# One Trainium2 kernel: x in two double loads, w1 in whole columns, and a new order of tasks

## The chip, the cores and the metric

The kernel runs on one core of one Trainium2 chip. Its work is spread over engines that run side by side: PE (TensorE, matrix multiplications; its weight loads are shown as PEld), DVE (VectorE), ACT (ScalarE), POOL (GpSimd) and SP (SyncE, which here only starts transfers). The metric is device time in microseconds, lower is better. A time is the median of several executions; the profile is one more execution, recorded by the hardware profiler.

## The reference

Two branches act on the same x of 2048 tokens by 512 features, in bfloat16, and are mixed by a gate per token:

```python
x = A_x
g = sigmoid((x * gate_w).sum(-1, keepdims=True))
X = rfft2(x)                       # over tokens and features
a = irfft2(X * (w_r + 1j * w_i))   # spectral filter, w of 2048 x 257
h = x @ w1 + b1                    # 512 -> 1792
b = (h * tanh(softplus(h))) @ w2   # 1792 -> 512; the activation is Mish
out = g * a + (1 - g) * b
```

## The kernel before

**Tiles.** x is cut into 16 tiles of 128 tokens; tile t holds the tokens 16p+t for p from 0 to 127. The dense branch goes by four groups c of four tiles and 14 column slices ft of 128 hidden units. Task `m{c}_{ft}` (line 847) is four matmuls of 128x512, one for each quarter of the 512 features, into one PSUM bank; `h{c}_{ft}` (line 852, ACT) applies bias and Mish and so frees the bank. For c = 0 and ft below 4 the task is split in two halves, `ma0_ft` and `m0_ft`, two matmuls each. `n{t}` (line 865) is the second layer for one tile, 14 matmuls; `o{t}` (lines 879, 882) scales it by 1-g.

**The spectral branch.** The transforms are written as matrix products. `bf{a}_0` and `bf{a}_1` (line 586, DVE) add and subtract the two halves of the features of the tiles of one x load. `p{t}` (line 604, PE) transforms along the tokens of a tile, `ep{t}` (line 501 on DVE, 504 on ACT) moves two tiles' results from PSUM to SBUF. `d{g}` (line 619) with `ed{g}` transforms along the features and needs all `ep`. `t{q}` (line 698, 64 small matmuls) combines the 16 tiles, `et{q}{h}` evacuates. The filter follows on DVE: `hp` (line 717), `p1` (720), `ad` (724) with the weights that `w?m`, `w?c`, `w?n` and `w?z` (lines 646 to 671) have spread out in SBUF; `w?n` copies 64x4160, and `wrz1` writes behind `wrn1` and so waits for it. `e1`, `xp`, `ead`, `e2`, `e3` treat one left-over frequency. Then the way back: `it` (line 780) with `eit`, which needs `e3`; `id` (819) with `ec` and `ey` (827, 830); and `ip` (873, 888), which adds the spectral result to the output, for tiles 8 to 15 inside the bank of `n{t}`. `fin` (892) adds the rest, `out` stores.

**The gate.** `graw` loads the gate row; `gt{t}` (line 593, DVE) multiplies it into a tile of x and sums; `zcl`, `ez`, `ez1`, `omg` and `gc` make the factors.

**The front.** `warm` and `fl` are matmuls on constants whose results nobody uses. The first four tiles reach the first layer through PE: `tr{t}` (line 573) transposes, `evx{t}` evacuates. Tiles 4 to 15 are transposed by the transfer `xt{t}`. `tr_b` and `ev_b` do the same for the bias; `tab` makes ACT load the table of Mish.

**What sets the order.** Nothing is scheduled while it runs. `ORDER` (line 329) is one long text; each engine takes its tasks in the order of that text, `name:engine:bank`. An engine may be chosen there, and the digits are PSUM banks (or the slot of a temporary). `place` (line 232) derives from it the waits: on the data, and on the last users of the same bank. So each engine is a queue in which a waiting task holds up all behind it. Loads go out from SP in the order of the text, and each waits until the load six places before it has landed (`KOUT`, line 20). The load groups stand in two constants:

```python
W1P = ((0, 2, 0, 4), (2, 4, 0, 4), (0, 4, 4, 8), (0, 4, 8, 11), (0, 4, 11, 14))   # k0, k1, first slice, end
XP = ((0, 1), (1, 2), (2, 3), (3, 4), (4, 8), (8, 12), (12, 16))
```

`w1_8_0` is the load of w1 for slices 8 to 10, all four feature quarters. In the text of before, the first layer begins with halves of slices 0, 2, 1, then 1 and 2, and then slice 8.

Of the kernel before, what the change touches and what calls it, by code (L numbers as in the profile page):

```python
# [333 lines left out]
p13 bf8_0 ep12:act bf8_1 gt11 m0_13::0 h0_13 m0_11::1 h0_11 wi0s1 m0_12::3 h0_12 p8::6 p9 ep8:act xt10 gt1 p10::4 p11 ep10:dve m1_9::2 h1_9 wr0s2  # L334
m1_12::0 d8::6 d9 xt15 h1_12 xt8 gt8 ed8:act d0::4 d12::2 d13 xt11 ed12:act gt4 xt9 gt9 xt13 gt10 ldM1 wr0s0 m1_4::1 d1 ed0:act wr0s1 d4::6 d5 ed4:act
xt14 m1_13::0 m1_2::2 h1_4 wi1s0 d10::4 d11 ed10:act h1_2 wi1s1 ldM2 d2::6 gt0 d3 m1_8::3 h1_8 m1_5::1 h1_5 gt2 d14::4 gt6 gt15 gt3 zcl d15 ed14:act
wim010:dve m1_3::2 h1_3 ed2:dve m1_10::3 xt12 h1_10 wim011:dve wim000:dve wim001:dve wic0:dve t0::64 d6::1 ez win0:dve h1_13 d7 wr1s0 et00:act
et01:dve wr1s1 m1_0::3 wiz0 hp01_1::1 hp00_1::2 ed6:act m2_2::0 h2_2 hp00_0 h1_0 hp01_0 w2_10 m2_7::6 h2_7 t1::41 et10:act et11:act hp11_0::0 m2_10::7
hp11_1 h2_10 ldM3 m1_1::0 w2_0 m2_5::3 h2_5 wrm000:act m2_0::6 wrm011:dve wrm010:dve ldG2 wrm001:dve wrc0:act c01 m1_7::4 wrn0:dve wrz0 ez1 omg c00
p1_01 m2_9::5 p1_00 m1_6::1 h1_6 h2_0 wim100:dve h1_1 wim101:dve m2_6::2 ad_01 hp10_1::1 m2_3::7 w2_5 ldG0 m2_1::3 h2_1 h2_3 m2_4::1 h2_4 wim111:dve  # L340
m2_11::6 h2_11 hp10_0 h2_6 p1_11 m2_8::0 m1_11::3 h2_8 wim110:dve h2_9 t2::61 et20:act m3_2::0 m2_12::5 m3_6::6 et21:act ad_11 h2_12 m3_1::7 m3_7::1
m2_13::2 p1_10 wic1:act h1_11 wrm111:dve h1_7 wrm101:act wrm100:dve h2_13 m3_12::5 wrm110:dve wrc1:act h3_1 h3_2 m3_0::3 ad_10 wrn1:dve edge ldG1 h3_6
m3_10::4 win1:dve wiz1 ldG3 m3_11::2 h3_11 m3_13::7 h3_0 h3_13 h3_12 wrz1 c02 m3_8::0 hp20_0::0 h3_10 hp20_1 m3_5::6 hp21_0::1 h3_7 m3_9::2 m3_3::3
h3_9 m3_4::7 h3_4 ad_00 hp21_1 p1_21 t3::41 ad_21 et30:act hp30_0::2 n3_0::7 et31:act c03 hp30_1 p1_30 p1_20 h3_3 e1::4 ad_30 xp20::1 h3_8 o3_0:act
ad_20 h3_5 n2_0::5 n0_0::1 xp1::2 xp21 ead::0 e2::2 o0_0:act hp31_1::1 hp31_0 n1_0::3 o1_0:act p1_31 ad_31 rft e3 it5_0::6 it2_0::0 it2_1 it5_1 inv
eit5:act n5_0::4 o5_0:act ezb zt::2 eit2:dve it1_0::0 o2_0:dve it1_1 zte it0_0::6 it0_1 eit0:act zw zr eit1:act it3_0::2 it3_1 eit3:dve n6_0::5
it4_0::6 it4_1 it7_0::3 it7_1 o6_0:dve it6_0::1 it6_1 eit6:act n9_0::0 rfs eit4:dve eit7:act id0::1 id14::6 id15 ec14:act:2 ey14_1 id1 ec0:act:0
id2::4 id3 ec2:act:1 ey0_0 n7_0::3 ey14_0 ey2_0 id10::6 id11 ey2_1 o7_0:act ey0_1 id8::4 id9 ec8:dve:2 ey8_1 id6::1 ec10:act:1 ey10_0 n4_0::3 o4_0:act
ey8_0 ip9_0 ey10_1 id12::4 id7 id13 ec12:dve:0 ey12_1 id4::6 id5 ec4:dve:2 ec6:act:1 n8_0::3 ip8_0 ey6_1 o9_0:act ey6_0 n10_0::0 o8_0:act ey4_0 ip1::1
# [600 lines left out]
```

## Time and profile before

| what | us |
|---|---|
| median of 3 runs | 132.89 (131.75 to 133.75) |
| the profiled execution, its own time | 131.67 |
| its span, first to last instruction | 130.1 |
| PE busy | 124.7 |
| DVE busy | 92.8 |
| ACT busy | 74.0 |
| bytes moved by transfers | 16.88 MB |

The profile tells, for each engine, when an instruction ran and what ended the wait ahead of it. The chain of work that ended last is followed back from the last instruction, at each step to what released it. A line number is that of the kernel's text. Matmuls overlap by their pipeline, so the pitch from start to start is what a matmul costs; its recorded length is longer.

### The profile page before, as it was taken

How to read it: one execution, taken by the hardware profiler on the slowest of the kernel's cores; microseconds unless marked ns; L12 is line 12 of the kernel's file. 1: busy time of each engine (PE TensorE's matmuls, PEld its weight loads, DVE VectorE, ACT ScalarE, POOL GpSimd, SP SyncE). 2: the span in 40 equal slices, each digit the busy share in tenths (PEclk: the TensorE clock that was granted, in tenths of full speed). 3: DMA queues.
4: the chain of work that ended last, by engine and by line, in shares of the span. 5: the costliest groups of instructions: out<-in, count | busy, mean ns of one | idle time of the engine just before them, and what ended most of it. 6: DMA issues, size and time to landing. Idle time of an engine off the chain costs nothing.

```text
span 130.1 us, 2561 instructions
## 1 busy us (share of the span) xinstructions
PE 124.7 (96%) x1076; PEld 65.2 (50%) x1076; DVE 92.8 (71%) x161; ACT 74.0 (57%) x105; POOL 4.7 (4%) x8
## 2 busy tenths in 40 slices
PE   7969999999999999999999999999999999999991
PEld 4624566665654445444454445556645544444440
DVE  0853797999995899999999996337098692803720
ACT  3852989999999879998959024354432520000202
POOL 2000000000470000000000000000000000000000
PEclk9999999999999999999999999999999999999999
DMA  3889998866799969998400002010000002000591
GB/s 109 247 255 367 316 134 282 126 99 67 198 212 140 262 108 292 363 375 274 166 5 0 0 0 55 0 72 10 5 0 0 5 0 81 0 0 0 187 337 40
DMA packets 17302, 16.88 MB, mean 130 GB/s; under 512 B 7628, under 2 KB 14668, under 8 KB 17228
## 3 DMA queue, kind: packets, MB, share of 16 engines
q1 hardware_dynamic: 17120, 16.60, 51.4%
q8 instruction: 8, 0.13, 0.4%
q10 hardware_dynamic: 172, 0.13, 0.3%
q14 instruction: 2, 0.02, 0.1%
HBM read 13.05 MB, written 2.10 MB: 116 GB/s over the span
## 4 chain that ended last, share of the span: by engine, by line
PE 56%; DVE 28%; ACT 5%; DMA 5%; SPq 2%; issue 2%; DVEq 0%
PE ps L865 28%; PE ps L847 14%; DVE rE L724 8%; DVE tmp L717 6%; DMA w_sb<-in_B_w_dram 5%; DVE rC L720 4%; PE ps L819 3%; PE ps L780 3%; PE ps L619 3%; SPq L467 2%; ACT rC L504 2%; DVE rW L649 2%; PE ps L604 2%; DVE rW L661 2%; PE ps L873 1%
## 5 line engine op out<-in xcount | busy, mean ns | idle before, releaser
L847 PE MATMUL ps<-rX,w_sb 128*128 128x512 bf16 x224 | 50.8, 379 | 1.5 <-DMA w_sb<-in_B_w_dram 1.5
L847 PEld LDWEIGHTS ps<-rX,w_sb 128*128 128x128 bf16 x224 | 21.1, 98 | 25.3 <-DMA w_sb<-in_B_w_dram 2.0
L879 ACT ACTIVATE rX<-ps,omg 128x512 bf16<-128x512 f32 x10 | 6.9, 687 | 37.4 <-PE ps L873 22.6
L865 PE MATMUL ps<-w_sb,hs 128*128 128x512 bf16 x112 | 25.2, 379 | 0.0
L852 ACT ACTIVATE hs<-ps,b1f 128x512 bf16<-128x512 f32 x28 | 18.2, 708 | 4.7 <-PE ps L847 3.6
L865 PEld LDWEIGHTS ps<-w_sb,hs 128*128 128x128 bf16 x112 | 10.5, 98 | 11.9
L865 PE MATMUL ps<-w_sb,rD 128*128 128x512 bf16 x56 | 12.8, 379 | 0.0
L865 PE MATMUL ps<-w_sb,rS 128*128 128x512 bf16 x56 | 12.6, 379 | 0.0
L830 DVE TENSOR_TENSOR rA<-tmp,ps 128x512 bf16<-128x512 f32 x16 | 10.0, 681 | 3.4 <-PE ps L819 3.4
L717 DVE TENSOR_TENSOR tmp<-rC,rA 64x1024 bf16<-64x1024 bf16 x16 | 10.8, 685 | 1.9 <-ACT rC L504 1.4
L504 ACT ACTIVATE rC<-ps 128x1024 bf16<-128x1024 f32 x11 | 11.4, 1060 | 1.0 <-PE ps L698 0.6
L586 DVE TENSOR_TENSOR rB<-rA 128x256 bf16<-128x256 bf16 (+1 forms) x14 | 5.9, 458 | 6.7 <-DMA rA<-in_A_x_dram 6.6
L593 DVE SCALAR_TENSOR_TENSOR rA<-rA,tmp 128x512 bf16<-128x512 bf16 x16 | 10.0, 688 | 0.2
L724 DVE TENSOR_TENSOR rE<-rC,tmp 128x1024 bf16<-128x1024 bf16 x8 | 9.8, 1224 | 0.3
L852 ACT ACTIVATE rD<-ps,b1f 128x512 bf16<-128x512 f32 x14 | 9.0, 692 | 0.9 <-PE ps L847 0.9
L852 ACT ACTIVATE rS<-ps,b1f 128x512 bf16<-128x512 f32 x14 | 8.6, 689 | 1.4 <-PE ps L847 1.4
L892 DVE SCALAR_TENSOR_TENSOR rX<-ps,gcol,rX 128x512 bf16<-128x512 f32 x8 | 5.6, 744 | 5.1 <-PE ps L888 5.1
L865 PEld LDWEIGHTS ps<-w_sb,rS 128*128 128x128 bf16 x56 | 5.5, 98 | 6.6
L882 DVE TENSOR_SCALAR rX<-ps,omg 128x512 bf16<-128x512 f32 x6 | 4.5, 747 | 5.8 <-PE ps L873 4.0
L865 PEld LDWEIGHTS ps<-w_sb,rD 128*128 128x128 bf16 x56 | 5.4, 98 | 6.2
L501 DVE CAST rC<-ps 128x1024 bf16<-128x1024 f32 x5 | 6.0, 1222 | 2.0 <-PE ps L604 2.0
L504 ACT ACTIVATE rF<-ps 128x1024 bf16<-128x1024 f32 x5 | 4.9, 1022 | 3.8 <-PE ps L780 3.8
(77 smaller groups left out, 113.9 us busy)
## 6 DMA issues: line engine op xcount, KB each, us to landing
rF<-c_m SPq DMA_DIRECT2D x4, 512.0 KB, 7.1
rB<-c_g SPq DMA_DIRECT2D x4, 512.0 KB, 7.8
out_dram<-rX SPq DMA_DIRECT2D x7, 256.0 KB, 2.4
rA<-in_A_x_dram SPq DMA_DIRECT2D x3, 512.0 KB, 6.8
w_sb<-in_B_w_dram SPq DMA_DIRECT2D x2, 640.0 KB, 10.3
w_sb<-in_B_w_dram SPq DMA_DIRECT2D x2, 512.0 KB, 8.9
rS<-in_A_w_i_dram SPq DMA_DIRECT2D x3, 257.0 KB, 6.5
rS<-in_A_w_r_dram SPq DMA_DIRECT2D x3, 257.0 KB, 8.4
```

The source lines that it names most:

```text
L501: return e.tensor_copy(out=o(), in_=i())
L504: return e.activation(o(), i(), AF.Copy)
L586: return e.tensor_tensor(out=xu[:, a:b_, uv, :], in0=x_sb[:, a:b_, 0:256], in1=x_sb[:, a:b_, 256:512], op=ALU.add if uv == 0 else ALU.subt ...
L593: t_gt.append(G.add(f"gt{t}", [("dve", 0.6, lambda e, t=t: e.scalar_tensor_tensor(out=x_sb[:, t, :], in0=x_sb[:, t, :], scalar=1.0, in1=tb ...
L717: return e.tensor_tensor(out=z3(z)[lo], in0=y3[hi], in1=wi3[hi], op=ALU.mult)
L724: return e.tensor_tensor(out=Yhq[:, q, h], in0=v(yv), in1=v(tb(z)), op=ALU.add)
L830: return e.tensor_tensor(out=yb[:, t:t + 2, 256 * h:256 * h + 256].rearrange("p t (i e) -> p t i e", e=2), in0=t4(z), in1=o4(bank(b, 1)), ...
L847: ins = e.matmul(bank(b), w1_sb[:, dt_, 128 * ft:128 * (ft + 1)], xT[:, c, dt_, :, :], start=(dt_ == 0), stop=(dt_ == 3))
L852: G.add(f"h{c}_{ft}", [("act", act(512, 1), lambda e, c=c, ft=ft, b=b: e.activation(hs[c][:, ft, :], bank(b), AF.Mish, bias=b1f[:, ft:ft + ...
L865: ins = e.matmul(bank(b)[:, 0:hi - lo], hs[c][:, ft, 128 * tl:128 * (tl + 1)], w2_sb[:, ft, lo:hi], start=(ft == 0), stop=(ft == NFT - 1 a ...
L879: return e.activation(bs[:, t, lo:hi], bank(b)[:, lo:hi], AF.Copy, scale=omg[:, t:t + 1])
L892: return e.scalar_tensor_tensor(out=bs[:, t, :], in0=bank(b), scalar=gcol[:, t:t + 1], in1=bs[:, t, :], op0=ALU.mult, op1=ALU.add)
```

## The change

The first four tiles of x come in two loads of two tiles, each with its own pair of butterflies (`bf0`, `bf2`) on 128x512. w1 comes in four loads that each hold all feature quarters of their slices: 0 and 1, 2 to 5, 6 to 9, 10 to 13. The gate row goes out behind the last of these loads. The opening run has 13 matmuls instead of 8, and the two `fl` stand apart. `tab` stands ahead of the first evacuation. All else is a new order: other places, other banks, and another engine for 33 tasks (among those that go to ACT `wrn1`, `wrm110`, `ep0`, `ep2`, `ep6`, `ep10`; among those that go to DVE `evx1`, `evx3`, `ep12`, `ep14`, `ed6`, `et11`). The instructions' number changes by the eight smaller butterflies that become four larger ones, by the opening run, and by the loads.

```diff
-W1P = ((0, 2, 0, 4), (2, 4, 0, 4), (0, 4, 4, 8), (0, 4, 8, 11), (0, 4, 11, 14))
-XP = ((0, 1), (1, 2), (2, 3), (3, 4), (4, 8), (8, 12), (12, 16))
+W1P = ((0, 4, 0, 2), (0, 4, 2, 6), (0, 4, 6, 10), (0, 4, 10, 14))
+XP = ((0, 2), (2, 4), (4, 8), (8, 12), (12, 16))
...
 ORDER = """
-warm::0 fl0::1 fl1::2 ones ident x1 bf1_1 x0 bf0_0 bf0_1 x3 bf3_1 bf3_0 tr1::3 cRF braw evx1:act tr_b::4 x2 bf1_0 w1_0_0 bf2_1 w1_0_2 w1_8_0 ev_b
-bf2_0 tr0::5 tr3::6 p0::0 tr2::7 evx2:dve p1 ep0:dve x4 p2::2 p3 evx3:act w1_4_0 x12 evx0:act ma0_0::4 ma0_2::6 graw::0 ma0_1::5 m0_1 tab w1_11_0 x8
-h0_1 m0_2 xt4 xt7 ep2:dve h0_2 xt5 m0_8::7 h0_8 bf4_1 ma0_3::0 bf4_0 m0_3 m0_9::1 h0_9 m0_0 xt6 h0_0 cFD p6::2 h0_3 p7 ep6:dve bf12_0 ldM0 m0_7::5
-h0_7 wi0s0 bf12_1 gt12 m0_4::6 h0_4 p4::0 m0_6::7 p5 h0_6 gt14 wi0s2 p14::3 ep4:act m0_10::2 gt13 p12::5 p15 ep14:act ebase m0_5::7 gt5 gt7 h0_10 h0_5
...
+braw warm::0 ones ident fl0::1 x2 ebase tab bf2_1 cRF x0 tr_b::2 ev_b bf2_0 tr2::3 evx2:dve w1_0_0 tr3::4 evx3:dve w1_2_0 x4 p2::6 x12 w1_6_0 tr0::5
+evx0:act tr1::0 bf0_0 x8 w1_10_0 p3 fl1::1 graw::0 xt4 bf0_1 p0::2 p1 evx1:dve ma0_0::4 m0_0 ep2:act ma0_1::1 ep0:act h0_0 xt7 bf4_1 xt5 ma0_3::5 xt6
+m0_1 m0_3 ma0_2::0 m0_2 h0_1 m0_4::6 cFD ldM0 bf4_0 p6::2 h0_3 p4::4 bf12_1 h0_2 m0_5::7 h0_5 p7 ep6:act wi0s0 bf12_0 p5 ep4:act m0_9::1 wi0s2 wi0s1
+m0_7::0 bf8_1 p12::2 h0_9 p13 m0_8::7 bf8_0 xt10 ep12:dve h0_7 h0_4 h0_8 p14::4 gt15 m0_10::1 p8::2 p9 p15 wr0s2 xt15 gt6 gt14 p10::6 xt8 h0_10
+ep8:act m0_6::0 gt2 xt11 ep14:dve xt9 m0_11::1 xt13 h0_6 p11 ep10:act gt5 m1_8::2 h1_8 m1_2::3 h0_11 h1_2 m1_0::0 h1_0 d12::4 d13 ed12:act d0::6 ldM1
+m1_13::2 h1_13 d1 d10::0 d11 gt13 ed10:act ed0:act m0_12::3 h0_12 wr0s0 m1_4::4 d4::1 h1_4 d5 gt8 ed4:act wr0s1 m1_7::5 d14::6 gt10 d15 gt11 ed14:act
+xt14 h1_7 m1_10::0 m1_12::3 h1_12 wi1s0 d2::1 d3 gt1 h1_10 wi1s1 ed2:act gt4 gt0 d8::6 gt3 gt9 gt7 gt12 wim001:dve wim011:dve zcl wim000:dve d9
+ed8:act d6::4 d7 m1_5::3 h1_5 m1_9::0 m1_3::1 wim010:dve wic0:dve win0:dve ed6:dve ldM2 ez ez1 omg h1_9 t0::64 et01:act wiz0 xt12 m2_12::2 wr1s0
+et00:act h2_12 m2_4::3 h2_4 hp01_1::1 m2_13::0 h2_13 hp01_0 wr1s1 h1_3 hp00_1::2 m2_6::4 h2_6 t1::62 et10:act hp00_0 et11:dve hp11_0::0 hp11_1 m2_8::5
...
+t2::63 et21:act win1:dve p1_11 m2_11::2 wrm111:dve p1_01 ad_11 wrm100:dve m3_3::5 wiz1 w2_5 et20:act m1_1::0 h1_1 m3_7::3 ldG0 h2_5 ad_01 m2_7::4 h2_7
+c02 h2_11 t3::60 et30:act et31:act wrm101:dve wrm110:act edge h3_3 h3_7 hp10_1::2 hp31_0::0 m3_0::4 h3_0 hp10_0 m3_12::2 p1_10 ad_10 hp20_0::1 hp20_1
+wrc1:act m3_10::6 wrn1:act ldG1 hp21_1::2 hp31_1 ldG3 m3_8::7 h3_12 m3_13::0 h3_13 m3_5::1 h3_8 wrz1 n1_0::5 o1_0:act zt::3 h3_5 hp21_0 p1_21 n0_0::4
+o0_0:act c03 p1_31 m3_4::2 h3_4 ad_21 m3_11::0 h3_11 p1_20 ad_20 e1::7 xp20::2 xp1::1 m3_1::5 h3_1 m3_6::1 h3_10 h3_6 m3_2::4 ad_31 n3_0::2 m3_9::0
+h3_9 xp21 ead::0 e2::5 h3_2 hp30_0::1 hp30_1 p1_30 ad_30 inv e3 n2_0::6 o2_0:act it3_0::0 it3_1 rft o3_0:dve zte zw zr it5_0::4 it5_1 eit5:dve
+eit3:act n5_0::7 it4_0::2 it4_1 it6_0::0 it6_1 eit4:dve eit6:dve it2_0::5 it2_1 eit2:dve n6_0::4 o6_0:dve it7_0::2 it7_1 o5_0:act it1_0::0 it1_1
+eit1:act it0_0::6 it0_1 n9_0::5 eit7:act eit0:act id6::0 id7 id10::3 id11 ec10:dve:2 ey10_1 id8::6 id9 ec8:act:0 n11_0::2 ey8_1 rfs ey8_0 ip9_0 ey10_0
+o9_0:act id12::6 id13 ec12:act:1 ey12_0 id14::3 id15 ec14:act:0 ey14_1 n8_0::5 ip8_0 ec6:act:2 ey6_1 ey6_0 ey12_1 o8_0:act ip11_0 ey14_0 id0::0 id1
...
+fin7 out13 ip0::3 fin3 out14 fin0 out1 n4_0::7 o4_0:dve ip4::2 fin4 out5 n15_0::0 ip15_0 o15_0:act out3 out7 out15:act
...
-def _build(nc, A_x, A_w_r, A_w_i, B_x, B_w1, B_b1, B_w2, gate_w, out, merge=8, xtp=XTP, NWARM=8):
+def _build(nc, A_x, A_w_r, A_w_i, B_x, B_w1, B_b1, B_w2, gate_w, out, merge=8, xtp=XTP, NWARM=13):
```

More of the change, by code (lines that the diff above doesn't have):

```diff
@@ L334 @@
[L334 to L349, printed above, removed]
@@ new lines @@
+xt14 h1_7 m1_10::0 m1_12::3 h1_12 wi1s0 d2::1 d3 gt1 h1_10 wi1s1 ed2:act gt4 gt0 d8::6 gt3 gt9 gt7 gt12 wim001:dve wim011:dve zcl wim000:dve d9
+ed8:act d6::4 d7 m1_5::3 h1_5 m1_9::0 m1_3::1 wim010:dve wic0:dve win0:dve ed6:dve ldM2 ez ez1 omg h1_9 t0::64 et01:act wiz0 xt12 m2_12::2 wr1s0
+et00:act h2_12 m2_4::3 h2_4 hp01_1::1 m2_13::0 h2_13 hp01_0 wr1s1 h1_3 hp00_1::2 m2_6::4 h2_6 t1::62 et10:act hp00_0 et11:dve hp11_0::0 hp11_1 m2_8::5
+h2_8 w2_10 m2_3::0 h2_3 wrm001:act wrm011:dve m0_13::1 h0_13 m2_2::4 ldM3 ezb c01 m2_0::6 h2_0 m2_10::7 wrm000:dve c00 wrm010:dve wim111:dve wrc0:dve
@@ new lines @@
+o9_0:act id12::6 id13 ec12:act:1 ey12_0 id14::3 id15 ec14:act:0 ey14_1 n8_0::5 ip8_0 ec6:act:2 ey6_1 ey6_0 ey12_1 o8_0:act ip11_0 ey14_0 id0::0 id1
+ec0:dve:2 o11_0:dve id2::6 id4::3 id3 ec2:act:1 ey2_1 ey2_0 id5 ec4:dve:0 gc n14_0::5 ip14_0 ip2::2 ip7::6 ey0_0 n12_0::7 fin2 ey4_0 ey4_1 ip12_0
+o12_0:act ip6::2 n10_0::3 ip10_0 ip3::4 n13_0::7 ip13_0 ey0_1 o13_0:dve fin6 o14_0:act ip5::0 out9 fin5 o10_0:act ip1::1 fin1 n7_0::5 o7_0:act out11
+fin7 out13 ip0::3 fin3 out14 fin0 out1 n4_0::7 o4_0:dve ip4::2 fin4 out5 n15_0::0 ip15_0 o15_0:act out3 out7 out15:act
```

4 lines of the change are left out of this document (1 added, 3 removed).

## The prediction

> **What bounds the kernel now.** First the page's totals, then the busy time by stretch (windows cut where one stage gives way to the next).
>
> ```profile
> span 130.1 us, 2561 instructions
> ...
> PE 124.7 (96%) x1076; PEld 65.2 (50%) x1076; DVE 92.8 (71%) x161; ACT 74.0 (57%) x105; POOL 4.7 (4%) x8
> ```
> ```profile
> 16.26:33.66 17.40, 17.40 (x151) 10.46 (x149) 16.30 (x41) 17.06 (x23) 0.11 (x1) 1.00 0.82 140
> 33.66:79.50 45.84, 45.75 (x461) 22.28 (x460) 42.14 (x65) 34.56 (x52) 3.90 (x1) 1.00 0.70 167
> 79.50:127.50 48.00, 47.93 (x377) 24.84 (x377) 25.98 (x39) 12.21 (x17) 0.00 (x0) 1.00 0.14 51
> 127.50:130.10 2.60, 0.00 (x0) 0.00 (x0) 0.00 (x0) 0.69 (x1) 0.00 (x0) 1.00 0.15 50
> ```
>
> After the length of a window come PE, PEld, DVE and ACT. From 16.26 to 127.5 us PE has work all the time, and the tail of 2.6 us holds one evacuation (ACT, 0.69) and a store. So TensorE bounds the kernel, and a new order can gain only ahead of about 10 us. But ACT is 98% busy from 16 to 34 us and DVE 92% from 34 to 79.5: an order that leaves either late costs PE time at once.
>
> Now PE's timeline, and the chain of work that ended last (start, length, what).
>
> ```profile
> 0.83 1.87 PE L517 MATMUL ps<-const-bfloat16-1.0 128*128 128x256 bf16 x8 [0.83 <-PEq L935]
> 2.49 0.63 PE L525 MATMUL ps<-const-bfloat16-1.0 128*128 128x256 bf16 x2
> ...
> 3.53 0.19 PE L563 MATMUL ps<-identt,rD 14*128 14x14 bf16 x1
> ...
> 6.19 2.32 PE L847 MATMUL ps<-rX,w_sb 128*128 128x512 bf16 x10
> 10.05 3.19 PE L847 MATMUL ps<-rX,w_sb 128*128 128x512 bf16 x14 [1.54 <-DMA w_sb<-in_B_w_dram]
> ```
> ```profile
> 4.11 5.89 DMA w_sb<-in_B_w_dram
> ...
> 13.24 0.45 PE ps L604 x8
> 13.69 1.73 PE ps L847 x8
> ...
> 33.73 1.00 PE ps L698 x64
> ...
> 40.90 0.69 DVE tmp L717
> ...
> 44.48 0.34 ACT rW L668
> ...
> 53.55 0.71 DVE rA L649
> ...
> 59.59 1.24 DVE rW L661
> ...
> 79.03 0.44 DVE rE L767
> ...
> 79.53 1.07 PE ps L780 x16
> 80.60 3.02 PE ps L865 x14
> ```
>
> Pitches: a first-layer matmul 0.216 us (1.73/8), so a column group of four 0.864; four matmuls of p or d 0.224; a second-layer tile 3.02. Ten first-layer matmuls from 6.19 are issued by 8.35; the eleventh, in column 8, starts at 10.05 because `w1_8_0`, issued at 4.11, took 5.89 us. That is 1.70 us start to start, the one large hole.
>
> **The change, part by part.**
>
> *The first matmul.* Removed: four x loads and eight half-size butterflies. Added: two double loads and four butterflies on 128x512.
>
> ```profile
> 0.79 1.34 SPq L467 DMA_DIRECT2D rA<-in_A_x_dram  x3
> ...
> 3.12 1.46 SPq L467 DMA_DIRECT2D w_sb<-in_B_w_dram  x3
> ...
> 5.17 0.43 SPq L467 DMA_DIRECT2D w_sb<-in_B_w_dram  x1
> ...
> 11.32 5.34 SPq L466 DMA_TRANSPOSE rX<-in_A_x_dram  x4
> ```
> ```profile
> 2.96 0.29 DVE L586 TENSOR_TENSOR rB<-rA 128x256 bf16<-128x256 bf16 x1 [2.96 <-DMA rA<-in_A_x_dram]
> ...
> 5.49 0.42 DVE L501 COPY rX<-ps 128x512 bf16<-128x512 bf16 x1
> 5.83 2.35 DVE L501 CAST rC<-ps 128x1024 bf16<-128x1024 f32 x2
> ```
>
> One tile landed at about 2.96 (DVE starts on it), and three were issued by 2.13. The first pair therefore lands between 2.96 and 3.5; I take 3.2. The second is issued third (0.45 apart), near 1.70, and lands near 4.1. Then DVE is the queue: `bf2_1`, `ev_b`, `bf2_0`, `evx2`, `evx3`, `bf0_0`, `bf0_1`, `evx1`. `ev_b` needs `tr_b`, which now stands behind 13 opening matmuls and one filler at 0.21 each (2.49-0.83 = 1.66 for eight): PE reaches it at 0.83+14x0.207 = 3.73 instead of 3.53, and `ev_b` starts near 4.0. From there seven operations follow at 0.34 (5.49 to 5.83; butterflies of 512 lie between 0.29 and 0.69, so nearer the first): `evx1` ends near 6.2, the first layer starts at 6.35 instead of 6.19: **+0.16** (bounds -0.2, +0.6). The longer opening run hides under this queue.
>
> *The hole.* The new list runs column 0 and half of column 1, six matmuls, up to 7.65, then column 3 from `w1_2_0` (512 KB). As far as the rows show, loads landed in order, and when several are queued their steps are short: `w1_4_0`, issued at 5.17, landed 7.5 us later.
>
> ```profile
> L467 SPq DMA_DIRECT2D w_sb<-in_B_w_dram x1: 432/432/432, 5.2 to 5.2; - x1
> ...
> DMA to landing us min/median/max: 7.5/7.5/7.5
> ```
>
> That is 12.7, against 11.32 for x4 (the transposes waited for it): 1.4 us for 512 KB. `w1_0_0` has 256 KB in rows of 512 bytes, an unseen form: between half of 1.4 and all of it; I take 1.0. Landings are then 4.1, 5.1, 6.5: the weights lie there 1.1 us before PE asks. **-1.70**. If one step stretches as `w1_8_0` did (from w1's second half at 3.60+3.2 = 6.8 to 10.0, 3.2 instead of about 1.05, +2.15), PE stands for 2.15-1.15 = 1.0.
>
> ```profile
> L467 SPq DMA_DIRECT2D w_sb<-in_B_w_dram x1: 468/468/468, 3.6 to 3.6; - x1
> ...
> DMA to landing us min/median/max: 3.2/3.2/3.2
> ```
>
> Continuing at 1.4 each, x4, x12, `w1_6_0`, x8, `w1_10_0` land near 7.9, 9.3, 10.7, 12.1, 13.5. PE wants p6 at 10.7 (after 14 more matmuls), column 9 at 12.4 (four p and a group later), column 10 at 15.7: no wait. The gate row follows at 13.9; its first user on DVE, behind the butterflies and `ep12`, comes near 16. Transposes wait for loads which land up to 3 us earlier, so the rest of SP's queue shifts forward. The second table load that falls away stood on ACT while the first layer's output was still due: 0.
>
> *From the first layer to t0.* 24 column groups and 28 p or d tasks: 24x0.864+28x0.224 = 27.0, PE is there at 33.4 (33.66 before).
>
> ```profile
> 25.23 3.84 ACT L504 ACTIVATE rE<-ps 128x1024 bf16<-128x1024 f32 x4
> 28.85 0.80 ACT L852 ACTIVATE hs<-ps,b1f 128x512 bf16<-128x512 f32 x1
> ...
> 47.65 4.16 ACT L852 ACTIVATE rD<-ps,b1f 128x512 bf16<-128x512 f32 x7 [0.74 <-PE ps L847]
> ```
>
> ACT's pitches are 0.905 for an evacuation ((28.85-25.23)/4) and 0.58 for a Mish. ACT waits for column 5, which PE ends at 12.1, until 12.25, then has 17 Mish and 11 evacuations up to `ed8`, whose bank t0 needs: 9.9+10.0, plus 0.5 waiting for p11, gives 32.7. Slack 0.7.
>
> *The move of `wrn1` to ACT.* DVE loses 1.24 us; ACT gets a copy of 64x4160 that no row shows.
>
> ```profile
> L504 ACT ACTIVATE rC<-ps 128x1024 bf16<-128x1024 f32 x11 | 11.4, 1060 | 1.0 <-PE ps L698 0.6 <-PE ps L619 0.3
> ...
> L646 ACT ACTIVATE rW<-rS 32x2064 bf16<-32x2064 bf16 x2 | 3.8, 1917 | 0.0
> ```
>
> From 1060 ns at 1024 to 1917 at 2064 is 0.82 ns per element: 3.64 us; in proportion to the second, 3.86. I take 3.65. Behind it on ACT wait `h3_12` and all later Mish, on DVE `wrz1` and `p1_21`. From t3's end PE has six groups (5.18) before n1 needs column 3's bank; ACT has there a leftover Mish, two evacuations, one 1.92 copy and `h3_3`: 4.9, slack 0.3. Then PE runs n1 and n0 (6.04+0.15) while ACT does two Mish, a 0.34 copy, `wrn1` and `h3_12`: 5.4, slack 0.8.
>
> *DVE up to it.* Before, 40.90 to 79.47: 38.57. New, from t1's end at 38.9 (33.4, t0, four groups, t1): `et11` moves in (+1.2, as half of the 2.35 above), `wrn1` and one 0.70 copy move out (-1.94), and `wrz1` waits about 0.4 for ACT: 38.9+1.2+36.63+0.4 = 77.1. PE has from 6.35: 56 groups (48.4), 28 p and d (6.3), four t (4.0), four second-layer tiles (12.1), edge and gate (0.3): 77.45. So DVE keeps up with 0.3 in hand, and the wait before 79.53 goes: **-0.29**.
>
> ```profile
> 76.22 3.18 PE L865 MATMUL ps<-w_sb,hs 128*128 128x512 bf16 x14
> ```
>
> (76.22+3.02 = 79.24 was due.)
>
> *After it.* The work is the same. Two places are without slack: n8 takes the bank of n9, whose evacuation now runs beside id12 to id15, and id4 takes that of `ey14_0`. Together 0.1 to 0.4. The tail stays: last tile, evacuation, store. For all the slacks under 0.5 I add **+0.5**.
>
> **Sum.** +0.16-1.70-0.29+0.5 = -1.33. The profiled execution took 131.67 us (span 130.1, 1.57 around it), so 130.3; the median shown, 132.89, lies 1.22 above it, and I carry that over: 131.5.
>
> **Rivals.**
>
> *The hole moves to `w1_2_0`.* A single load gates twenty matmuls; the trace shows one stretched step among the first nine, which speaks for it, and the earlier issue (fifth, near 2.65, against 4.11) against. +1.0 to +1.3: 132.7.
>
> *ACT becomes the bound between 12 and 34 us* (other side). The place is t0's wait for `ed8`, and the bound moves once ACT's 28 operations take over 0.7 us more than summed. If the 11 evacuations go at their mean length, 1.06, because each waits for its own pair of matmuls and no longer overlaps, they cost 1.7 more: 1.0 late at t0. The same pitch in the four later evacuation pairs and in the ten of the it and id stages adds up to 1.6 where their slack is 0.3. -1.33+2.6 = +1.3: 134.2. For it: ACT gains some 5.6 us of work over the kernel (`wrn1`, one 1.92 copy and one evacuation more, two x evacuations less). Against: in the same stretch before, evacuations did run at 0.905.
>
> *The clock.* The opening matmuls (256 columns in 0.207) run at half the pace of 0.216 for 512, and by 6.19 the pace is full, so PE needed at most 5.4 us of work to get it. Between about 4.4 and 6.3 the new order gives PE little; if it falls back there, the next 3 to 5 us run at half pace: +1.7 to +2.5 for the half of it that is lost, 133.6. Against: a hole of 1.54 left the 14 matmuls behind it at full pace (3.19). The Trainium skill, "TensorE: Matmul & The Clock Gate", Part 1, has the clock halve only after an idle window of some 3.4 us and open after as much sustained work; the trace agrees as far as it goes, and by that rule the longer opening run gains nothing either.
>
> *The run-to-run part goes too.* The runs shown spread from 131.75 to 133.75, above the profiled one. If that is lateness of the first loads, the 1.1 us in hand absorbs most of it: 130.2.
>
> **How the numbers follow.** Forecast 0.50 (own range 130.8 to 132.4); hole moves 0.18; ACT 0.17; clock 0.03; run-to-run part goes 0.12. Two per cent, about what a measurement of this kernel can tell from no change, are 130.2 and 135.5. Half of the last case and a little of the forecast's low edge are faster: 0.10. Slower needs ACT late in nearly every stage, a third of its case, or something unseen: 0.10. The range cuts the last case at its better half, 0.5 below its centre, and the ACT case just above its centre: 129.7 to 134.4.
>
> **What would show it.** Right: first-layer matmuls from about 6.4 without a hole over 0.3, t0 near 33.4, the first `it` near 77.5, the last evacuation near 126.2. Wrong: an idle time before L846 put down to w_sb, PE gaps ending on ACT between 12 and 34 us, or a gap at `m3_4` after the long ACT copy. Most of all, a chain that leaves PE between 13 and 33 us would break the sum.

## The result and the profile after

The changed kernel took 130.84 us (median of 12 runs, 130.38 to 131.28); the kernel before, run beside it, 131.72 (12 runs, 131.42 to 133.75). The ratio is 0.9924, 95% interval 0.9898 to 0.9950: a small gain, no difference by the bound of 2%. (The ratio leaves out executions over 1.5% above the fastest of their kernel, so it is not quite the quotient of the medians.) The forecast was 131.5 in a range of 129.7 to 134.4, with 0.80 on no change. Against the median of before as it was then known, 132.89, the forecast was -1.39; what came is -0.88.

The profiled execution, the second fastest of the twelve, took 130.5 us (before 131.67), its span 129.3. The page's totals:

```profile
span 129.3 us, 2565 instructions
...
PE 125.2 (97%) x1081; PEld 66.0 (51%) x1081; DVE 89.6 (69%) x156; ACT 78.0 (60%) x105; POOL 3.7 (3%) x8
```

TensorE is still the bound, with 97% of a shorter span. The table of stretches (after a window's length come PE, PEld, DVE, ACT, POOL, then granted clock, share of the DMA engines, GB/s):

```profile
16.69:34.42 17.73, 17.73 (x147) 10.45 (x144) 17.03 (x42) 17.14 (x25) 1.54 (x1) 1.00 0.67 151
34.42:78.96 44.54, 44.54 (x451) 21.57 (x451) 39.64 (x63) 37.76 (x50) 1.38 (x1) 1.00 0.69 164
78.96:126.62 47.66, 47.66 (x377) 24.79 (x375) 25.65 (x37) 11.81 (x17) 0.00 (x0) 1.00 0.12 41
```

From 16.69 us to the last matmul PE has no idle time, although ACT is 97% busy up to t0 and DVE 89% from there to the first `it`. What there is to explain inside the span lies in the first 14 us. (Column n of w1 is slice n.) PE's timeline:

```profile
0.83 2.93 PE L516 MATMUL ps<-const-bfloat16-1.0 128*128 128x256 bf16 x13 [0.83 <-PEq L934]
...
5.34 0.62 PE L572 MATMUL ps<-identt,rA 128*128 128x128 bf16 x8 [0.18 <-DMA rA<-in_A_x_dram]
...
6.15 0.62 PE L603 MATMUL ps<-rD,rB 128*128 128x128 bf16 x8
6.61 4.73 PE L846 MATMUL ps<-rX,w_sb 128*128 128x512 bf16 x20
...
13.42 1.90 PE L846 MATMUL ps<-rX,w_sb 128*128 128x512 bf16 x8 [0.33 <-DMA w_sb<-in_B_w_dram]
...
75.94 3.18 PE L864 MATMUL ps<-w_sb,hs 128*128 128x512 bf16 x14
78.96 1.06 PE L779 MATMUL ps<-rB,rE 128*128 128x128 bf16 x16
```

The first layer starts at 6.61 (6.19 before). Its first 20 matmuls, 4.32 at a pitch of 0.216, are followed by p6 at 11.17, 4.56 later: 0.24 of waiting within, ahead of column 3. Column 9 starts 0.50 late at 13.42 (p5 was issued at 12.70 and costs 0.22). The first `it` follows n2 at 75.94 + 3.02 = 78.96, without a wait. Start to start the two profiles differ so: start +0.42; hole 1.70 before, 0.24 + 0.50 now, -0.96; the wait before `it` -0.29; together -0.83. The last matmul ended at 127.46 before and ends at 126.62: -0.84. So inside the span of these two profiles nothing is left over.

But the two profiled executions differ by 1.17 us, and 0.33 of that lies outside the span, which runs from the first instruction to the last: 1.57 us before (131.67 - 130.1), 1.24 now (130.5 - 129.26). This is so in every execution whose span is on record: 1.46 to 1.63 around the span before, 1.20 to 1.28 in the twelve of the changed kernel. And the pair of profiles shows more gain in the span than is typical: the median span is 130.1 to 130.2 before (three sets of executions) and 129.6 in the twelve of the changed kernel. Of the gain of 0.88 about 0.6 therefore lies inside the span (the 0.29 ahead of `it` included) and 0.3 outside.

Where the loads stand, by their issue and their time to landing (first the load of w1's columns 6 to 9, then the x loads of tiles 4 to 7 and 12 to 15 together; each first line ends with the times of the first and the last issue, each last line has the shortest, middle and longest time from issue to landing):

```profile
L466 SPq DMA_DIRECT2D w_sb<-in_B_w_dram x1: 649/649/649, 4.2 to 4.2; - x1
...
DMA to landing us min/median/max: 9.1/9.1/9.1
```
```profile
L466 SPq DMA_DIRECT2D rA<-in_A_x_dram x2: 430/467/504, 3.2 to 3.8; - x2
...
DMA to landing us min/median/max: 6.2/7.2/8.1
```

Columns 6 to 9 land at 13.4 (4.2 + 9.1, rounded), where 10.7 was forecast. Tiles 4 to 7 land at 9.4 (3.2 + 6.2) and the next load, also 512 KB, only at 11.9: a step, from one landing to the next, of 2.5 us, where the three loads of this size behind it take 1.3 to 1.5 (columns 2 to 5, two places ahead, took 2.0). The first pair of tiles landed at 3.7 (2.9 after its issue), the second at 5.3, where 3.2 and 4.1 were taken. So PE's new order did not remove the wait for loads; it cut it from 1.70 to 0.74 and paid 0.42 at the start.

### The profile page after: what moved, and what is told of

Same layout as the page of the kernel before. It is cut to its first block, busy times and chain, and to the rows that moved or that the text cites. A ratio compares the mean times of both kernels' runs of the same rounds, so it can differ in the third digit from the quotient of the medians.

```text
span 129.3 us, 2565 instructions
## 1 busy us (share of the span) xinstructions
PE 125.2 (97%) x1081; PEld 66.0 (51%) x1081; DVE 89.6 (69%) x156; ACT 78.0 (60%) x105; POOL 3.7 (3%) x8
## 4 chain that ended last, share of the span: by engine, by line
PE 88%; DMA 7%; SPq 2%; ACT 1%; issue 0%
PE ps L864 38%; PE ps L846 34%; DMA w_sb<-in_B_w_dram 7%; PE ps L697 3%; PE ps L818 3%; PE ps L618 3%; PE ps L779 3%; SPq L466 2%; PE ps L603 1%; PE ps L872 1%; PE ps L887 1%; ACT rX L878 1%; PE ps L794 0%; PE ps L740 0%; PE ps L762 0%
## 5 line engine op out<-in xcount | busy, mean ns | idle before, releaser
L846 PE MATMUL ps<-rX,w_sb 128*128 128x512 bf16 x224 | 51.6, 379 | 0.4 <-DMA w_sb<-in_B_w_dram 0.3
L878 ACT ACTIVATE rX<-ps,omg 128x512 bf16<-128x512 f32 x11 | 7.5, 690 | 30.2 <-PE ps L872 19.8
L864 PEld LDWEIGHTS ps<-w_sb,hs 128*128 128x128 bf16 x112 | 10.7, 98 | 12.3
L503 ACT ACTIVATE rC<-ps 128x1024 bf16<-128x1024 f32 x13 | 13.2, 1060 | 0.9 <-PE ps L697 0.5
L585 DVE TENSOR_TENSOR rB<-rA 128x1024 bf16<-128x1024 bf16 (+1 forms) x10 | 5.5, 580 | 9.4 <-DMA rA<-in_A_x_dram 9.4
L716 DVE TENSOR_TENSOR tmp<-rC,rA 64x1024 bf16<-64x1024 bf16 x16 | 10.7, 685 | 0.6 <-ACT rC L503 0.2
L881 DVE TENSOR_SCALAR rX<-ps,omg 128x512 bf16<-128x512 f32 x5 | 3.8, 763 | 8.7 <-PE ps L872 7.8
L500 DVE CAST rF<-ps 128x1024 bf16<-128x1024 f32 x4 | 4.7, 1219 | 3.5 <-PE ps L779 3.5
L503 ACT ACTIVATE rE<-ps 128x1024 bf16<-128x1024 f32 x7 | 7.0, 1056 | 0.0
```

What stands on the lines that cost most here:

```text
L500: return e.tensor_copy(out=o(), in_=i())
L503: return e.activation(o(), i(), AF.Copy)
L585: return e.tensor_tensor(out=xu[:, a:b_, uv, :], in0=x_sb[:, a:b_, 0:256], in1=x_sb[:, a:b_, 256:512], op=ALU.add if uv == 0 else ALU.subt ...
L716: return e.tensor_tensor(out=z3(z)[lo], in0=y3[hi], in1=wi3[hi], op=ALU.mult)
L846: ins = e.matmul(bank(b), w1_sb[:, dt_, 128 * ft:128 * (ft + 1)], xT[:, c, dt_, :, :], start=(dt_ == 0), stop=(dt_ == 3))
L864: ins = e.matmul(bank(b)[:, 0:hi - lo], hs[c][:, ft, 128 * tl:128 * (tl + 1)], w2_sb[:, ft, lo:hi], start=(ft == 0), stop=(ft == NFT - 1 a ...
```

## The experiments

Ratios are to the kernel before, run in between on the same chip. Theory from the above: the gain comes from the front alone, and is what the load queue leaves of it. An edit to `ORDER` shows only the words around the change.

**Whole columns of w1 in the old order.**

```diff
-W1P = ((0, 2, 0, 4), (2, 4, 0, 4), (0, 4, 4, 8), (0, 4, 8, 11), (0, 4, 11, 14))
+W1P = ((0, 4, 0, 2), (0, 4, 2, 6), (0, 4, 6, 10), (0, 4, 10, 14))
...
-w1_0_0 bf2_1 w1_0_2 w1_8_0 ev_b
+w1_0_0 bf2_1 w1_2_0 w1_6_0 ev_b
...
-p3 evx3:act w1_4_0 x12
+p3 evx3:act x12
...
-tab w1_11_0 x8
+tab w1_10_0 x8
```

> The old order with the new w1 loads only (slices 0-1, 2-5, 6-9, 10-13; the load of slices 6-9 stands where w1_8_0 stood). Theory A: the stretched landing step belongs to the queue of loads, whichever load meets it; slice 8 now comes with 384 KB more ahead of it, so the hole before slice 8 grows from 1.70 to about 2.7 us and the kernel takes about 132.7 (+1.0). Theory B: the step belongs to w1_8_0 and its rows of 768 bytes; then w1_6_0 lands near 8.9, the hole shrinks to 0.6 and the kernel takes about 130.6 (-1.1).

Measured: 131.69 us, ratio 0.9985 (0.9962 to 1.0007). PE's timeline:

```profile
6.48 0.59 PE L847 MATMUL ps<-rX,w_sb 128*128 128x512 bf16 x2
8.37 4.92 PE L847 MATMUL ps<-rX,w_sb 128*128 128x512 bf16 x22 [1.30 <-DMA w_sb<-in_B_w_dram]
```

The hole goes from column 8 to column 2: the old order asks for column 2 after two matmuls, and the load that holds it is a whole 512 KB. A had it right that the wait goes with the queue, but not its place, and neither expectation had its size. Inside the span the loads alone bring nothing (its median is 130.3, before 130.2); they need an order that works on columns 0 and 1 first. The one load less does show outside the span: 1.33 to 1.41 us there, against 1.46 to 1.63 for the kernel before.

**The old loads, with columns 3 and 0 ahead of column 8.**

```diff
-m0_8::7 h0_8 bf4_1 ma0_3::0 bf4_0 m0_3 m0_9::1 h0_9 m0_0 xt6 h0_0 cFD p6::2 h0_3 p7
+bf4_1 ma0_3::0 bf4_0 m0_3 m0_0 h0_0 h0_3 m0_8::7 h0_8 m0_9::1 h0_9 xt6 cFD p6::2 p7
```

> The old kernel with one edit: in front, slices 3 and 0 (six matmuls, their weights already landed) go ahead of slice 8. Theory A (the change's gain is the filled hole and nothing else in the new order): the hole of 1.70 shrinks to about 0.4 and the kernel gains 1.0 to 1.3, about 130.5, as much as the whole change or more. Theory C (the gain comes from the new places further on, DVE's lighter chain ahead of the it stage above all): PE arrives earlier but waits for DVE before it, gain under 0.4, about 131.5.

Measured: 131.31 us, ratio 0.9975 (0.9952 to 0.9999).

```profile
6.68 5.34 PE L847 MATMUL ps<-rX,w_sb 128*128 128x512 bf16 x24 [0.25 <-DMA w_sb<-in_B_w_dram]
12.60 0.62 PE L604 MATMUL ps<-rD,rB 128*128 128x128 bf16 x8 [0.58 <-DVE rB L586]
```

The hole before column 8 is gone, and the next load in the queue is late instead: p6 waits 0.58 for the butterflies of tiles 4 to 7, the start 0.25 for w1. Of 1.70 us some 0.3 to 0.5 remain as gain (0.3 by the ratio, 0.5 by the medians), between what A and C had said. It is the same picture from the other side: take one wait away, and PE reaches the next load too early.

**A short opening run in the changed kernel.**

```diff
-def _build(nc, A_x, A_w_r, A_w_i, B_x, B_w1, B_b1, B_w2, gate_w, out, merge=8, xtp=XTP, NWARM=13):
+def _build(nc, A_x, A_w_r, A_w_i, B_x, B_w1, B_b1, B_w2, gate_w, out, merge=8, xtp=XTP, NWARM=8):
```

> The new kernel with 8 opening matmuls instead of 13. Theory A (the first landing at 3.71 and the queue on DVE behind it set the start of the first layer): no difference to the new kernel, 130.8 within 0.2. Theory D (the longer run buys the full clock early): PE stands idle from 2.7 to 3.7, transposes and the first matmuls run at half pace for longer, 0.5 to 1.7 slower than the new kernel, 131.3 to 132.5.

Measured: 131.14 us, ratio 0.9956 (0.9928 to 0.9984), 0.3 us above the changed kernel, with overlapping intervals: between the bands of A and D.

```profile
3.28 0.19 PE L562 MATMUL ps<-identt,rD 14*128 14x14 bf16 x1 [0.38 <-DMA rD<-in_B_b_dram]
3.71 1.04 PE L572 MATMUL ps<-identt,rA 128*128 128x128 bf16 x8 [0.24 <-DMA rA<-in_A_x_dram]
...
6.52 1.06 PE L603 MATMUL ps<-rD,rB 128*128 128x128 bf16 x8
7.38 4.68 PE L846 MATMUL ps<-rX,w_sb 128*128 128x512 bf16 x20
...
13.65 1.89 PE L846 MATMUL ps<-rX,w_sb 128*128 128x512 bf16 x8
```

Two idle times of 0.62 together stand where the five matmuls were, and eight matmuls of p take 1.06, against 0.62 in the changed kernel: PE runs at half pace up to 7.4 and the first layer starts 0.77 later. But then it waits for no load, and column 9 starts only 0.23 later. In this execution the late start is taken back almost whole by the waits; but at 130.73 us it was the fastest of its twelve.

**Four single loads of x in the changed kernel.**

```diff
-XP = ((0, 2), (2, 4), (4, 8), (8, 12), (12, 16))
+XP = ((0, 1), (1, 2), (2, 3), (3, 4), (4, 8), (8, 12), (12, 16))
...
-tab bf2_1 cRF x0 tr_b::2 ev_b bf2_0 tr2::3
+tab bf2_1 x3 bf3_1 cRF x0 x1 tr_b::2 ev_b bf2_0 bf3_0 tr2::3
...
-tr1::0 bf0_0 x8
+tr1::0 bf0_0 bf1_0 x8
...
-xt4 bf0_1 p0::2
+xt4 bf0_1 bf1_1 p0::2
```

> The new kernel with the first four x tiles in four loads, each with its own small butterflies on DVE. Theory A (loads and small butterflies about balance: tiles land 0.5 earlier, DVE has four more operations of 0.21 to 0.29 in the same queue): first layer at 6.5 to 6.7 as now, 130.8 within 0.3. Theory E (the late landing of the double loads, 3.71 and 5.30, is what the front lost against the forecast): first layer near 6.2, 0.4 faster, 130.4.

Measured: 131.62 us, ratio 0.9985 (0.9965 to 1.0005): nearly all of the gain is gone.

```profile
6.90 1.46 PE L846 MATMUL ps<-rX,w_sb 128*128 128x512 bf16 x6 [0.31 <-DMA w_sb<-in_B_w_dram]
8.51 3.19 PE L846 MATMUL ps<-rX,w_sb 128*128 128x512 bf16 x14 [0.16 <-DMA w_sb<-in_B_w_dram]
...
14.37 1.90 PE L846 MATMUL ps<-rX,w_sb 128*128 128x512 bf16 x8 [0.90 <-DMA w_sb<-in_B_w_dram]
```

The single tiles land earlier (the second pair at 4.4 and 5.1 instead of 5.3), but w1 goes out two issues later, and its three loads all keep PE waiting. Column 9 starts at 14.37, 0.95 later; the time is 0.8 longer, of which about 0.1 lies outside the span (1.33 to 1.43 there).

**Columns 6 to 9 ahead of the x load of tiles 12 to 15.**

```diff
-x4 p2::6 x12 w1_6_0 tr0::5
+x4 p2::6 w1_6_0 x12 tr0::5
```

> The changed kernel with one pair swapped in the load queue: column 6 to 9 of w1 ahead of the third x load (tiles 12 to 15). Theory A (what is left of the hole is a late landing of one load in the queue, and PE has the next work ready): the 0.50 us before column 9 (13.42, load landed 13.37) go, because the load lands one place earlier, by 12.0; the x load lands near 13.4, its butterflies end near 14.9, p12 (15.16) still finds them; last matmul 0.4 to 0.5 earlier, near 126.15, time 130.3 to 130.5. Rival B (the queue moves the wait, as it did when whole columns were put into the old order): p12 waits for the butterflies of tiles 12 to 15, which now land with the stretched step, and the time stays at 130.8 within 0.2.

Measured: 130.5 us (130.22 to 131.11), ratio 0.9902 (0.9878 to 0.9926), the lowest here. Like the changed kernel's, its interval lies below 1; against the changed kernel the intervals overlap.

```profile
7.15 4.77 PE L846 MATMUL ps<-rX,w_sb 128*128 128x512 bf16 x20 [0.28 <-DMA w_sb<-in_B_w_dram]
...
13.51 1.89 PE L846 MATMUL ps<-rX,w_sb 128*128 128x512 bf16 x8
```

Column 9 waits no more, and no p waits for its butterflies, as A had it. But in this execution the first load of w1 was late, the start is 0.54 later, and column 9 starts at 13.51 all the same: the last matmul came at 126.71, not 126.15. The median moved by what A said, this profile does not show it. Nor did the long step stay with its place in the queue: columns 6 to 9 now took 1.3, and the x load of tiles 12 to 15 behind them 1.65.

**`wrn1` back on DVE.**

```diff
-m3_10::6 wrn1:act ldG1
+m3_10::6 wrn1:dve ldG1
```

> The changed kernel with the long copy wrn1 put back from ACT (3.66 us there) to DVE (1.24). Theory A (both engines are beside PE, with 0.8 us in hand on each): DVE takes 1.24 us and loses its 0.75 wait for ACT, so its last step before the inverse (e3, 78.15) comes 0.5 later, 0.3 before PE asks (78.96); no PE gap, time as the changed kernel within 0.15 (130.7 to 131.0). Rival B (the move of this copy is what removed the 0.29 wait before the first it task): that wait comes back, first it task at 79.2 or later, time 131.1.

Measured: 130.83 us, ratio 0.9921 (0.9889 to 0.9952). The copy on ACT and what DVE waited for, in the changed kernel; then DVE and PE without the move:

```profile
62.31 3.67 ACT L663 ACTIVATE rW<-rW 64x4160 bf16<-64x4160 bf16 x1
```
```profile
66.15 0.09 DVE L670 MEMSET rW<- 128x32 bf16 x1 [0.75 <-ACT rW L663]
...
77.71 0.44 DVE L766 CAST rE<-ps 128x64 bf16<-128x64 f32 x1
```
```profile
63.77 1.23 DVE L660 TENSOR_SCALAR rW<-rW 64x4160 bf16<-64x4160 bf16 x1
...
77.94 0.44 DVE L766 CAST rE<-ps 128x64 bf16<-128x64 f32 x1
```
```profile
78.62 1.06 PE L779 MATMUL ps<-rB,rE 128*128 128x128 bf16 x16
```

DVE ends `e3` at 78.38, 0.24 before PE asks: A, nearly to the tenth. A task of 1.23 us goes from one engine to the other, where it takes 3.67, and the time stays, because both are beside PE. So the 0.29 did not go through this move; which of the others removed it was not tried. It belongs to the new order all the same: in the four profiles with the old one PE stands idle for 0.11 to 0.14 ahead of the first `it`, in the ten with the new one never, however late the front was.

**Two more evacuations on ACT.**

```diff
-ep12:dve
+ep12:act
...
-ep14:dve
+ep14:act
```

> The changed kernel with two more evacuations on ACT between 15 and 21 us (ep12 and ep14, on DVE before). They add 2 x 0.96 us there; ACT's own gaps behind them (0.12, 0.07, 0.40) take 0.59 back, so ACT is 1.3 us later from ep10 on. Theory A (ACT had 0.54 us in hand at t0, as the trace says): PE waits for ACT between 24 and 35 us, t0 at 35.2 instead of 34.42, the last matmul and the time 0.8 later: 131.6. Rival B (ACT is loosely tied there, and the stretch from 12 to 34 us was never near a bound): under 0.2 later, 131.0. Rival C (lateness on ACT repeats in each of the later stages, as the forecast's second rival had it): over 1.9 later, 132.8 or more.

Measured: 131.97 us, ratio 1.0016 (0.9990 to 1.0042), 1.1 to 1.5 above the other versions of the changed kernel run beside it.

```profile
19.14 0.40 PE L603 MATMUL ps<-rD,rB 128*128 128x128 bf16 x4 [0.80 <-ACT hs L851]
...
35.73 0.46 PE L697 MATMUL ps<-rE,rF 32*128 32x128 bf16 x20
```

Column 9 starts at 13.38, as in the changed kernel; then p10 waits 0.80 for a Mish that ACT now ends late, and t0 comes at 35.73 instead of 34.42, 1.3 later. A had the mechanism and 0.8; it had overlooked that p10 takes over the bank of `h0_4`, one of the Mish behind the first moved evacuation. The last matmul ends 1.3 later too: the lateness goes through once and is not repeated, and C falls.

**A transposing load moved.** The transposing load of tile 13 now stands ahead of those of tiles 4 to 7.

```diff
-graw::0 xt4 bf0_1
+graw::0 xt13 xt4 bf0_1
...
-m0_11::1 xt13 h0_6
+m0_11::1 h0_6
```

> The changed kernel with the transposing load of tile 13 put ahead of those of tiles 4 to 7. It waits for the x load of tiles 12 to 15, so no transposing load is issued before that has landed; in the changed kernel the first one was issued at 9.43, just when the next load took 2.47 us to land (9.41 to 11.88) where a queued 512 KB otherwise takes 1.3 to 1.5. Theory A (writing out the transposing load slows the loads in the queue): the step shrinks to 1.5, column 9 lands near 12.4 and its 0.50 wait goes; the transposes of tiles 4 to 7 end about 1 us later, near 21, in front of their first user or at most 0.5 behind: 130.4 to 130.9. Rival B (the slow step has nothing to do with it): a step of over 2 us is still there, the 0.50 wait stays: 130.8 to 131.3.

Measured: 130.71 us, ratio 0.9917 (0.9897 to 0.9937). The edit did not do what the expectation says. SP's queue:

```profile
9.95 8.54 SPq L465 DMA_TRANSPOSE rX<-in_A_x_dram  x5
```

The first transposing load went out at 9.95, as soon as the load six places before it had landed, and not behind tiles 12 to 15: it reads x in DRAM and waits only by `KOUT`. The expectation had that wrong, and whether these loads slow the others is not settled by it. Other profiles show that a slow step needs none of them: `w1_8_0` took its step of 3.2 before the first transposing load went out (11.32), and columns 2 to 5 in the changed kernel their 2.0 (8.09, against 9.43). The profile here is of use all the same, by PE's timeline:

```profile
6.21 0.62 PE L572 MATMUL ps<-identt,rA 128*128 128x128 bf16 x8 [0.72 <-DMA rA<-in_A_x_dram]
...
7.46 4.48 PE L846 MATMUL ps<-rX,w_sb 128*128 128x512 bf16 x20
...
13.54 1.68 PE L846 MATMUL ps<-rX,w_sb 128*128 128x512 bf16 x7
```

Here the second pair of tiles was late (6.2) and the first layer started at 7.46; then PE waited for no load, and column 9 stood at 13.54, 0.12 behind the first profile. A late start and a wait on the way are one and the same lateness of the loads, paid once.

**The gate row in its old place.**

```diff
-x12 w1_6_0 tr0::5
+x12 graw::0 w1_6_0 tr0::5
...
-fl1::1 graw::0 xt4
+fl1::1 xt4
```

> The changed kernel with the gate row back in its old place in the load queue, behind the x load of tiles 12 to 15 and ahead of column 6 to 9 of w1. Theory A (what stands ahead in the queue costs its own step where PE waits for the load behind it): the row's step is 0.4 to 0.5 (0.38 before, 0.47 after), column 9 lands that much later; the last matmul and the time 0.3 to 0.5 later than the changed kernel's of this call. Rival B (landings vary so much from one execution to the next that the place of a 128 KB load drowns in it): within 0.15.

Measured: 131.14 us, ratio 0.9974 (0.9942 to 1.0006), where the changed kernel as it is, run beside it, had 0.9952 (0.9916 to 0.9987): 0.36 later, as A says, with intervals that overlap. In its profile the gate row's step was 0.36, but PE had started late (7.58) and column 9 hardly waited. So A is likely, not shown.

**Four loads in flight.**

```diff
-KOUT = 6
+KOUT = 4
```

> The changed kernel with at most four loads from SP's queue in flight instead of six. Theory A (the slow landing steps come from how many queued loads share the engines): no step of a 512 KB load over 1.7, the waits ahead of columns 3 and 9 go, 0.4 to 0.7 faster than the changed kernel of this call. Rival B (they have another cause, and each load is still issued over 4 us ahead of its landing): steps over 2 us stay, time within 0.2. Rival C (the queue now runs dry, since a load needs over 2 us from issue to landing even alone): later landings, 0.5 or more slower, the transposing loads late as well.

Measured: 131.67 us, ratio 1.0010 (0.9984 to 1.0036), 0.9 above the changed kernel as it is (130.78, below).

```profile
9.09 3.20 PE L846 MATMUL ps<-rX,w_sb 128*128 128x512 bf16 x14 [1.13 <-DMA w_sb<-in_B_w_dram]
```

Rival C: columns 2 to 5 go out at 3.81 instead of 2.66 and land at 9.0; tiles 4 to 7 still need a step of 2.0. The transposing loads go out from 14.07 on instead of 9.43, and PE waits another 0.36 at 40.3 for a load of constants (`c_m`). Fewer loads in flight do not make the steps even; nor can a transposing load be the cause of that step, which ended at 11.0.

**Both kernels once more.** No edit in either.

> The changed kernel as it is, once more, for its landings in another execution and as the measure of the other runs of this call. Theory A (the slow step falls at another place in each execution, and the new order pays for it wherever it falls): a step over 1.9 us for another load than in the first profile (w1's columns 2 to 5 and the x load of tiles 12 to 15), column 9 between 13.0 and 13.6 all the same, t0 between 34.0 and 34.6; time 130.7 to 130.9. Rival B (the slow steps belong to places in the queue): the same two loads take 2.0 and 2.5 again.

> The kernel before as it is, once more, for its landings. Theory A (the slow step wanders in this kernel too): the load of columns 8 to 10 lands before 9 us, and the hole ahead of column 8 is under 0.8. Rival B (in the old queue the slow step belongs to that load, as in the two profiles with that queue so far, 3.23 and 2.47): it lands near 10 again, and the hole is 1.4 to 1.8.

Measured: the changed kernel 130.78 us (130.23 to 132.37), the kernel before, one execution, 132.28. The changed kernel's timeline in this execution, and the window of its slow part (the granted clock is the figure behind POOL):

```profile
4.02 1.03 PE L572 MATMUL ps<-identt,rA 128*128 128x128 bf16 x8
...
6.01 1.03 PE L572 MATMUL ps<-identt,rA 128*128 128x128 bf16 x8 [0.53 <-DMA rA<-in_A_x_dram]
...
7.48 1.06 PE L603 MATMUL ps<-rD,rB 128*128 128x128 bf16 x8
8.34 5.11 PE L846 MATMUL ps<-rX,w_sb 128*128 128x512 bf16 x20
...
15.04 1.89 PE L846 MATMUL ps<-rX,w_sb 128*128 128x512 bf16 x8
```
```profile
6.00:9.60 3.60, 3.58 (x24) 2.72 (x25) 1.18 (x3) 2.69 (x3) 0.00 (x0) 1.00 1.04 379
```

This execution took 132.13. PE was at half pace to 9.6 (the first three matmuls of the first layer cost 0.43 each), column 9 started at 15.04 and t0 at 36.04: 1.5 later than in the profile with the moved transposing load (34.54), where the second pair of tiles landed as late (6.2; here 6.0), but its eight transposes took 0.62 and not 1.03: there the pace was full by then. So my A was wrong on column 9: not only the loads vary, but also when PE gets its full pace. Tiles 12 to 15 took their long step (2.25) here too, columns 2 to 5 did not (1.45). The second pair took 1.96. So half of B holds, and half of A. In the kernel before the load that made the hole came early this time, as A says:

```profile
L467 SPq DMA_DIRECT2D w_sb<-in_B_w_dram x1: 467/467/467, 4.1 to 4.1; - x1
...
DMA to landing us min/median/max: 4.5/4.5/4.5
```
```profile
7.47 6.38 PE L847 MATMUL ps<-rX,w_sb 128*128 128x512 bf16 x24
```

It landed at 8.65 instead of 10.00, and there was no hole before column 8 at all. The execution was still no shorter than the first: a tile of x was late, PE started at half pace, and the first layer came at 7.47. The 1.70 us that the prediction was built on was the form that the lateness of the loads took in one execution.

## Why the prediction was right, and where it was wrong

**The bound.** Right. PE has hardly any idle time from 16 us on in either kernel (0.16 us before, none now), and what changed inside the span lies ahead of that, but for the 0.29.

**The first matmul** (+0.16, bounds -0.2 and +0.6): measured +0.42. The step that failed is the landing of the double loads, taken at 3.2 and 4.1; they landed at 3.7 and 5.3, the first above the upper bound of 3.5. The bound of 3.5 was read from tiles of 128 KB, which land 2.15 after issue; a pair took 2.9. DVE's queue was as said, one operation every 0.34, but it could start only at 3.73 and waited a little for PE's transposes:

```profile
4.67 0.75 DVE L500 COPY rX<-ps 128x512 bf16<-128x512 bf16 x2
5.35 0.75 DVE L585 TENSOR_TENSOR rB<-rA 128x512 bf16<-128x512 bf16 x2
```

It reached `bf0_0` at 5.35, 0.05 after the second pair had landed, so that both latenesses lead to the same start; `evx1` ended at 6.43, where 6.2 was taken. (The working counts seven operations behind `ev_b`; there are six, and its 6.2 fits six.) PE then still had p1 to issue ahead of the first layer.

**The hole** (-1.70): measured -0.96. This is the term that was mis-sized. Each landing was forecast with one short step after another from 5.1 on, and the 1.1 us in hand came out of that; columns 6 to 9 came 2.7 late: 1.2 from the x pairs, 0.6 from the step of columns 2 to 5 (2.0, where 1.4 was taken) and 1.1 from that of tiles 12 to 15 (2.5, where 1.4 was taken), less 0.2 on the load of columns 0 and 1. The prediction saw such a step and priced it at 1.0 as a rival. It should have been in the forecast: of fourteen profiles of either kernel and the variants, eleven have a step of 1.9 to 3.2 among the first eight loads, and in the other three the longest is 1.7 or 1.8. Typical executions gained less still: of the 0.6 by which the median span shrank, the 0.29 ahead of `it` leaves about 0.3 for the front (an estimate from these two figures), where the first two terms had forecast 1.54.

**The wait before `it`** (-0.29): right; and its reason, that DVE keeps up with 0.3 in hand, erred on the safe side (0.8 in hand, 0.24 without the move of `wrn1`). `wrn1` took 3.67 on ACT (3.65 taken) and DVE waited 0.75 for it (0.4 taken).

**The slacks** (+0.5): 0. No place that was listed made PE wait. The two errors, +1.00 in the front and -0.5 here, leave -0.83 instead of -1.33.

**The base.** Two things here were off, and both made the time come below the forecast although the gain in the span was smaller. The forecast carried over 1.22 us between the profiled execution and a median of three runs, two of which were late: with twelve runs the median of before is 131.72, 0.05 above the profiled one, and for the changed kernel the difference is 0.34. And it kept the 1.57 us around the span, without a reason, where the change has 1.24. In sum: the gain in the span 0.50 too large, the time around it 0.33 too long, the carry-over 0.88 too long; -0.71 together. That 131.5 lies within 0.7 of the result is thus in part luck, errors with opposite signs.

**The rivals.** The hole moved to columns 2 to 5 in the old order (1.30) and with four loads in flight (1.13), and in small (0.24) in the changed kernel: true as a mechanism, not in its full size. ACT had 0.5 us in hand up to t0, close to the 0.7 that was worked out, and the pitch of 0.9 held; two more evacuations were enough to turn the gain into nothing. The clock was priced at 3% and 133.6: the profile of 132.13 shows its lesser form, a pace that opens late instead of falling back, at +1.35 over the median. Of the eleven other executions of that set two more lie at 132.1 and 132.4; why is not known, as they have no profile. The last rival, 130.2, lies as near the result as the forecast does, but not for its reason: the 1.1 us in hand were not there, and the carry-over shrank because two of three runs of before had been late ones.

**The opening run** ("gains nothing"): probably wrong. With 13 matmuls full pace came by 6.2 us in eight of nine profiles, with 8 matmuls between 3.9 and 9.6 in five. Between two profiles it bought 0.77 at the start of the first layer, of which 0.23 was left at column 9; the 0.3 us in the medians are not clear of the noise. The Trainium skill, "TensorE: Matmul & The Clock Gate", Part 1, has full pace come about 4 us into sustained work, half a microsecond more or less; the traces agree in the main, with a wider spread: in seven of the nine profiles it came 2.7 to 4.5 us after the first matmul at 0.83, in one while PE stood idle between 5.3 and 6.2, and in the execution of 132.13 it had not come when PE fell idle at about 5.4, and came 3.6 us after it resumed. The likely error was to take it that the matmuls which come later anyway would do as well: without the five, PE stood idle twice for 0.62 us in all within that time, and full pace came only at 7.8.

## What to carry to other kernels

A hole that one profile shows before one load may be a sample of how late the loads are and no property of that load: look at a second execution, or price the move of the wait to the next load as the likely case and not as a rival. In a front that is fed by one queue, each load ahead costs its step to all behind it; order both the loads and the work by first use, and count what PE can do between landings. Work that only keeps PE busy before its data come is probably worth its place if it closes the idle times there. And compare medians of equally many executions of both kernels before a difference between one profile and a median is carried over; what lies outside the span of the profile belongs to the time as well.
